# Q, K and V of two batches loaded two rows to a partition, in an attention and MLP kernel on one core

## The chip, the core and the metric

The kernel runs on one core of a Trainium2 chip. The core has TensorE (matrix products), VectorE, ScalarE, GpSimd and SyncE, which run side by side, each through its own list of instructions in order, and 16 DMA engines that serve the loads and stores which SyncE, ScalarE and GpSimd issue. Products are written to PSUM, eight banks here; all else lies in SBUF, with 128 partitions. The metric is the time on the device in microseconds (us), less is better.

## What is computed

First comes an attention with selected chunks: 4 batches, 8 heads, 768 positions, 64 values per head. K is cut into 24 chunks of 32 positions. An upper bound of a query's scores in a chunk is computed from the chunk's minimum and maximum of K, the six chunks with the highest bounds are kept (causally), and the softmax runs over these alone. The result goes through an MLP of 512 to 2048 to 512 with ELU.

```python
k_min = np.min(k_chunks, axis=3)
k_max = np.max(k_chunks, axis=3)
ub = np.sum(np.maximum(q[:, :, :, None, :] * k_min[:, :, None, :, :],
                       q[:, :, :, None, :] * k_max[:, :, None, :, :]), axis=-1)
ub = np.where(causal, ub, -1000000000.0)
top_chunks = np.argsort(ub, axis=-1)[..., -top_k:]
scores = scale * np.matmul(q, k.transpose(0, 1, 3, 2))
mask = sel & (pos[:, None] >= pos[None, :])
scores = np.where(mask, scores, -1000000000.0)
...
return np.matmul(attn, v).astype(np.float32)
...
h = x @ w_in
g = np.where(h > 0.0, h, alpha * (np.exp(np.minimum(h, 0.0)) - 1.0))
return (g @ w_out).astype(np.float32)
```

Inputs and output are float32; the kernel's products of scores, values and MLP are bf16.

## The kernel before

The work is cut into eight units of 384 rows. Units 0 and 1 hold the first halves of batches 0 and 1, in two steps of 192 positions: step p (`u == 0`) takes positions 0 to 191 of both batches, where no selection is needed because there are at most six chunks; step s (`u == 1`) takes positions 192 to 383. `prep_pair` (L379) loads and prepares them, `score_first` (L679) has the scores of step p, `attend_pair` (L708) the rest. Units 2 and 3 are the second halves of batches 0 and 1, units 4 to 7 the halves of batches 2 and 3; `prep` (L514) and `attend` (L770) do these. `mlp` (L868) then does one unit: 16 groups of four products with w_in (L875), for each group an exp on ScalarE (`e`, L882), a step on GpSimd or VectorE (`m`, L884) and one on VectorE (`g`, L888), and then three row tiles of 16 products with w_out (L899).

Every piece is an operation of a graph (`g.op`), with the engines that may run it. Which engine runs it, in which order on each engine, and in which buffer its result stands, is written out in two strings, `ORDER` (L39) and `PLACES` (L103): three characters for each operation (an engine and a number), one for each buffer. No scheduler decides on the chip: each engine does its list in order, and an instruction that waits holds back all behind it. There are 40 products with zeros (`fill`, L938) in the order that serve no result.

In batches 0 and 1 K and Q come in with positions on partitions, are transposed on TensorE into PSUM (L408 and L548; f32), and go on as follows. VectorE takes the minimum and maximum of each chunk from the bank into `kst` (`bounds`, L369, instructions at L372), and a subtraction follows (L375). K is copied as bf16 into `kt` (two heads, one above the other, on 128 partitions), and from there each head's 64 rows into `lhs` (`ka`). Step p uses `kt` and a copy of Q (`xt`) for its scores directly. In the other steps Q goes to `qt`, its positive part to `qr`, and each head's half to `rhs` (`qa`). `lhs` and `rhs` also hold, in rows 64 to 95, a pattern of chunks (`econst`) and the mask of the selection, so that one product of 96 rows gives a masked score. V is cast to bf16 into `vext` (`vcast`).

`select` (L590) multiplies `kst` with `qt` and `qr` (L603), turns the bounds on VectorE (L614), takes the eight largest of each row's visible chunks (L622), compares (L627), turns back (L631) and copies the result into `rhs` (`mk`).

Batches 2 and 3 do it in another way (`keys`, `bounds_batch`): K is cast into `kt` in another layout, transposed by a DMA into `lhs`, and its bounds come from a separate load `kc`.

The loads of K for step p are issued from ScalarE's queue and SyncE's, all other loads of Q, K and V from SyncE's, the weights from GpSimd's. In each, the last axis of the array in HBM, 64 float32 or 256 bytes, is one contiguous piece, as in these lines of `prep_pair`:

```python
src[b, h0:h1, t0 + T96 * x:t0 + T96 * (x + 1)].rearrange("h p d -> p h d")
```

V and Q of step p are put into the place of w_out (`stage`), which is loaded later.

Of the kernel before, what the change touches and what calls it, by code (L numbers as in the profile page):

```python
# [9 lines left out]
AOT = mybir.AluOpType  # L10
# [6 lines left out]
H = 8  # L17
S = 768
D = 64
# [20 lines left out]
D01A0sS0tS0xS0XS0wA0uS2hS0YA0VG0iD00S0ZS0yS2fS0+S0vD09G0jA0rD03G0eG04PjFA0WA02P1aS2kD1bS0BP11PjG  # L40
G0aG0cP18PjIS2iPjKS2gD0-S0zP0MP0DD19D15PjHG0bA05A0QP1tP0TD0ED17A1eD1cS2QP1uP1vD1dD0kD0FD10PjMP0K
P1kA1wPjOD0HD12P1oP1pG0dS2vA0UPjJD0OD0qD06A0LG0GA0SD0lG0nP1zP1qG0fD0mD13P2oG0RPjLA1xP1hD0pPjQD0N
A1rD0oP1SG0CP1jP1RP1lA1sA16P2BD2pA1iA1nG0AP1yD2qGmjP1AA2FPjNP1XD2DA1mP1OD1TGmkP1NA1CD2rD2CS3fP2w
S2RP2JA2sP1HPjPD1PP1EA1BG07GmlD2xP1DP1ID1JP20PjSD1UA2uPjRS2PD1QP29A2KP2aPjTS2OP1YG2HG0JD1FP33P1+
S2VPjVS2mD14S2ID1KD1GA1fA2yD1ZP3gD21P1VP25D2bG2EPjUD2LA2GP1LP26D22G0PD1-D1MP23D2cD27D24A1WD28A34
P3lPjWP2dD3nD3mA36PjXD3pPjZA2eD3oD3qD3rS2TPmuD2NAmvG2AD3hG37G3sDmwPmKPmGPmOP3JG3uPmCPj+PjYPmqD2S
AmLG0IAmHP2XAmPA2tGmmDmMDmNA35PmyG08AmrGmIGmnDmxS32P38DmJPk1Pk3G3tA2+Pj-DmQPk0G3vD2YPk5Pk2A2zPk7
A3KD2ZAmzP3HD39AmDPnmS4-DmRS4YDmEPniDmFA3cGmAPm-D3aG3dPmSA3IAm+AnnGmsDmBGn0DmtP3+Pk4GnoPn6AnjPna
GnkA3iG2-Dn1DnpD3kGmoP41An7Gn8G2lAnbDnlA31A40PnDPk6PmWAmTPk8GncDn9PnwA2MPn2G3bDndP3wA42AmXGmUDmV
A2nGmYPnePnxD1gDmZPk9P4lD3yP4FS50G30A3jS4+P4DAn3G43GmpG2WPnED3AA4mGn4D3xD3zD3BD2jP4jA4EP45PnqPnr  # L50
# [12 lines left out]
P7EA7nS7hP7DD7FA82D7GSnIPoQGc-D7XPkaD86D89D87S7HP8pP8BA8CPoRG8xPoSA8qG8nA8rPpsA8yA8dG8sSaxD7WD8k
D8jD8DSbADoTAptPpAA8ePpwPpoGaOG7YG8aPaPG8lG8oD88P8GD7ZApBGpCApxGpuPpcDpDSayPpgDpvGpyDpzPp0G8EApp
Pp8D8IG8bD8HAaQD8KPp4GpqDprA7-AaSApdAphGpiD8JDpjAp1PpkGpeDpfGp2G8gDp3AaTG8zD8LPpQAaRAp9SoVAp5PpI
GpaGp6ApRDpbDp7AplPpUGpSAb7A7+DpTSavPpEPpMPpYG8tPqcD8MApJSawApFSc+Pq0GpKSaCGpmDpLDpnApNGpGDpHAb9
G8NP93P8ZGcUG8OGbaSaUApZAb6ApVDp-P91Dp+PqdDpOP97DpWP96A94A92P8XG8fScLP8+DpPPq1A8-G95A8YDaWDbfA98
G99G8QP8TP8VG8PP9xP9wA90Pq2ScKP8RA8WA8UP9jP9rA9yDd0DpXP9bDaVDbhDboA8SA9kG9zP9fP9lA9sP9tP9aP9pA9m
P9hG8AA9uD9vP9nA9qDbvG8FSbBA9iDbDPq3P9RA9oP9HP9XP9WSaEGcTA9gD9cP9TP9FPqeSbbDq4D9dP9BA9YD9ZSf4A9I
DcXA9SA9GDaBP9ASazA9UP9ND9CP9PD9DP9JPahPadPa7PabSaXA9OG9VSb8A9QA9KPalP9LA9MGhxPakPqfDaZP9-DaYPaf  # L70
P9+AaePkcAbwPa3Da-Sq5ScRAa8Da+AacPkeAamDqgPq6Pa5Da0AagDa1Aa4S9EAaiSfgGb0Aa6DajGanPa9Pq7PaoAbgAaa
PapS9eSoUDbFDbdAbESa2DaqDarPb1GbGAb4Pq8Ab2PkdSasDfiAb5GbcAb3PbHDbIPq9PkfAbyDbJSbeGbiGcWDbKPkgSf5
DbLDbqDbMGcSSf9PqqPqSDbNPqmDbxAd1AqaAqrPqiAqTPquAbPGqsGbOPbYGqUAqnPbXPqCScPPreDqtDqVGqoGbRDqpPca
PbSDfhAqvDdcGqwPc9AqjAbQAbZGqkAqDGqEAbTDqlDqxPq-PqKArfDqFSf3Pr6ScNPcoPcnGrgPcCAq+AcbAr7GaDPcBDd8
PqyGr0AcpPcwSqhPr2AcDAqzPbUGr8SgbDrhDaFDr9Ar3PqWPcyDr1GcqAcxPciPqGDddGqAGr4AbVAczShkGb-Sf6Sf7PqO
Pc6ScYGcODr5AqHAqXGqIGd2AcjDqBProDd4DqJPckSgcDqYSg2Pc4ShlPraDcAAqLSfjGqMAc7ScVGbWGcEDqNPriPrjAcl
Ac5ArbDfRAd9PcFAqPAhwAd6DcmPc0GccPcrSf8PcsDc8PcGPb+Ad3DqZPceDrcPcdDd5DcHPrpGqQDqRPrqDcfDcgDrdPdg
PruPrrPrkPrlDc1GdfAfODctDc2SchGdbDcIGfPSc3DcuScvPrvScJPrIPs4PrUSqbDdiDflDdhPrASg1ArmDdkDdjSg9AfL
DdlPrwGdeSfQArsAs5DdmArVDdnPdJPdtSrnDfkSfxGrWGs6AhtPrQSfaDrXDdoPdIPrxGd7Pe6Pe7DfmArJAduGrKDs7PdF
ArBDrLAdKArRGrCGrSPrMDrDPdBDhCPdvPrESg4Ae8ArNDrOAdwArFGdqDrTDrPPsoGrGPdrPs0PsgAdCDdLPdDDryPdxAsp  # L80
AdGPdRShnAs1DrHGsqPrYSrzDsrAdsAshDe9DhuGsiPdzAdyShyDdaSgaAdEAdSPswPdVPs8ShvAdADdpDsjDdHArZGcQGs2
PdZPe1AsxPdNPdMSfXDs3GfJDr-PexAdWGsySfYDszPssDdOGfIAs9SfWPe3Ae2Dr+PdTAd-Pd+PeXDdPPeWDhEAdUPewAey
Ae0Ae4AeYPsAAstPdXPscPsBDsaPskSrtPefSfKDezAdYDfnGsuDsbDe5PeaAsdAslPeTPebGseSfeSg3PepDsfDecPelPsC
DedSfVAegPetPehDsvAemGsmGfoPfpPerAeUDsnDfsPenAeqShrPeHDfzSdQDfyDgdGfMDfZDg5AeuPsDPeJAesPeLAeoAei
GevPsMAeMAfqPejPeNPeBAeKAekPeFPeADfSPeRGg8AeOPsNAeSAeIPePDeCDeVGhAPsGGeZDeDDfbAeGPe-SeeAeQPe+PsH
PsIGfUAftDf0PsOPsJGg7Df1AgeSfuSeEDsEDfwSf2Pt2DfvPs-PtKDfrAsKGffDf-DfADfBDfCPfDPt6PsSAt3Dt4DfEAtL
As+SsLPsPGgfGtMDg6AfGAfFDf+Gt0Dt5DfHPghDt1PsWAsTGsUSfNDtNPtaPtiDsVShpAt7AsXDgiSfcPtqAtbDgjShmDgk
GhFGggDglDgmGt8GsYPtGPtOGtcAtjDsZPtmAsQDgnGfTGtkDt9AtrGgoPgxPgyAtHDtdGtsAgqPtyPgZDtlPgsPg-SsRDtt
PgWDhKAtnAgzDgAGgrGtoGgpGg0PteAtPDtpAgXPtCDtIAg+GtQPguPgUDtJAgtPgGAtfAgVDhGPtYDtgPtuAtzDtRAgvAtv
GtADh0SsFPtSAtDPgIDhzAgJDthPtZPtTDtwGgwPgMDtxAfdDtBAgHGgYPh8PgLPgBPhbDhHGhNAgNPh2PhcDgKPt-DtEPh6  # L90
PgCGgOAh9PgQPh1PgPDtFDhODgDAhdPu2Pu3Ah7GhaDgEPtUSgFDgRDh3DhLDgSDhePhfPhgGhJAhDAhPPhSPtVShBAhRAho
GhIDhhDhiPt+Pu4SgTShjGhMDh4Sh5DhTPu5PucGhsPuIPv4DhUDhVPukAtWAudAhqAuJDhWAu0DhXDhYStXDhZAv5PuwPi7
PugDu6GueGh-PibAulGuKAi8Su7AuxGumDuLPidPu8GuyDunPuoDufPiBAicAieAuhPi1Gv6PuADuzDv7Pi3GuiAu9AiCPuQ
GuaAupAuBPi5DujPixDubPusAi4Ai6DuqPuEPiDAi2GhQDurAuRPi9PiJDuSAiyAutPveGuCPiIAiEAuFPijDuDDuTDuGPii
AiaPivPifPuUAiwDuHPiFAigDuuPuYPuMDuvPvfAuVDihAikAuNDilPimPinGuWPizDuXAi0AiGPv0AiKPitDh+DuODuPAuZ
PjwAv1PirPvgAiuDioDipPi+Pj1Gu-Gv2AiAPjxGiLDiHPiTDu+PiRDv3Aj0Pj6PvhAisAj2PiNPiXPiMPj7Pj3AjyAiUAj4
DjzPv8PiVDviPjtAiSAj8DiOPiZSiqPv9DiPAiYPjfDj9Ai-PjrAiWGj5PjnPjbPjlPjaPjjAjuDjcAjgAjsPjhSiQAjoDjv
AjmDjdPvkPjpPvlSvjAjiAjqAjkPjBPjADjCSjeSu1PvaPvbPvmPvnAvoDjDSjEPvqAvcPvOPvyPvCPwaPvuAvzAvDGvAPv-
# [889 lines left out]
```

## Time and profile before

| | us |
|---|---|
| three runs | 289.12, 288.97, 287.55 |
| median | 288.97 |
| profiled execution | 288.57 |
| its span | 286.7 |
| mean granted clock of TensorE | 0.994 |

The page of the profile shows one execution. Its span runs from the first to the last instruction. A group of instructions is named by line, engine, operation and tile, with its count, its busy time, and the mean of one in ns; after the bar stands the idle time of the engine before it and what ended it. PEld is TensorE's loading of weights, beside its products. Products overlap on TensorE, so the mean duration of one is longer than the distance between two. A helper's line (L325, L327, L251, L309) stands for many operations; the tiles tell them apart. A row of the stretches gives the busy us of each engine with the count of its instructions, then TensorE's granted clock, the mean busy share of the 16 DMA engines (over 1 where packets overlap on one engine) and GB/s.

### The profile page before, as it was taken

To read this page: it belongs to the slowest core of one execution; us is meant where nothing else is said; L and a number is where in the kernel's file an instruction comes from. 1 tells how busy PE (TensorE), PEld (TensorE's weight loads), DVE (VectorE), ACT (ScalarE), POOL (GpSimd) and SP (SyncE) were. 2 spreads that over 40 slices of the span, in tenths; PEclk is the share of its full clock that TensorE was granted. 3 is DMA by queue.
4 is the path that set the end of the run, shared out by engine and by line. 5 is a ranking of instruction groups with operands and counts; after the bars stand their busy time and mean duration, and the time that the engine had idled before them with its cause. 6 is when DMAs were issued, how large, how long until landed. Compare 5 with 4: busy or idle time off the path is not lost.

```text
span 286.7 us, 6781 instructions
## 1 busy us (share of the span) xinstructions
PE 262.3 (91%) x2373; PEld 160.9 (56%) x2404; DVE 225.6 (79%) x608; ACT 195.9 (68%) x441; POOL 148.0 (52%) x285
## 2 busy tenths in 40 slices
PE   0669899999999999998899999998999989999995
PEld 0547565585556755565455455664465446665653
DVE  0397997769999999999989999698999867631850
ACT  2167587588999866898599278973488369892631
POOL 5065389743787568965379335335486442310520
PEclk9997999999999999999999999999999999999999
DMA  8999999969994679675789569973820430013003
GB/s 153 191 200 200 205 202 225 212 134 214 200 173 143 123 154 209 89 154 162 115 188 226 105 155 203 181 127 85 182 76 2 94 74 0 16 51 116 23 1 112
DMA packets 119714, 39.25 MB, mean 137 GB/s; under 512 B 111104, under 2 KB 115456, under 8 KB 119680
## 3 DMA queue, kind: packets, MB, share of 16 engines
q1 hardware_dynamic: 113072, 33.80, 59.7%
q0 software_dynamic: 3696, 4.19, 8.5%
q10 hardware_dynamic: 2912, 0.82, 1.5%
q8 instruction: 19, 0.31, 0.5%
q14 instruction: 15, 0.12, 0.1%
HBM read 30.41 MB, written 6.29 MB: 128 GB/s over the span
## 4 chain that ended last, share of the span: by engine, by line
PE 48%; DVE 28%; DMA 9%; ACT 5%; issue 5%; POOL 2%; SPq 2%; DVEq 0%; ACTq 0%
PE bank L875 15%; PE bank L899 13%; DVE km L491 6%; PE bank L785 5%; DVE gT L888 4%; DMA xt<-on 4%; PE bank L836 3%; DMA f<-in_k_dram 3%; ACT e L882 3%; PE bank L603 2%; DVE on L649 2%; DVE kst L372 2%; PE bank L408 2%; DVE thr L622 2%; PE bank L548 2%
## 5 line engine op out<-in xcount | busy, mean ns | idle before, releaser
L875 PE MATMUL bank<-xt,w_in_sb 128*128 128x384 bf16 x512 | 92.7, 326 | 3.9 <-DMA xt<-on 2.6
L884 POOL TENSOR_SCALAR m<-e 128x384 f32<-128x384 f32 x99 | 52.7, 541 | 73.4 <-ACT e L882 57.0
L899 PE MATMUL bank<-w_out_sb,gT 128*128 128x512 bf16 x338 | 86.4, 379 | 1.8 <-issue 0.2
L882 ACT ACTIVATE e<-bank 128x384 f32<-128x384 f32 x128 | 60.4, 497 | 27.0 <-PE bank L875 22.5
L888 DVE SCALAR_TENSOR_TENSOR gT<-bank,m 128x384 bf16<-128x384 f32 x128 | 66.5, 549 | 11.1 <-POOL m L884 9.4
L800 ACT ACTIVATE pt<-bank 128x384 bf16<-128x384 f32 (+1 forms) x144 | 68.6, 551 | 4.5 <-PE bank L785 2.2
L875 PEld LDWEIGHTS <-w_in_sb 128*128 128x128 bf16 x512 | 49.1, 98 | 38.5 <-issue 6.2
L899 PEld LDWEIGHTS <-gT 128*128 128x128 bf16 x368 | 34.5, 97 | 34.7 <-issue 1.6
L785 PE MATMUL bank<-rhs,lhs 96*128 96x384 bf16 (+2 forms) x240 | 45.1, 293 | 0.4
L491 DVE TENSOR_REDUCE km<-kc 96x64 f32<-96x1024 f32 x16 | 30.5, 1918 | 0.1
L785 PEld LDWEIGHTS <-lhs 96*128 96x128 bf16 x240 | 21.9, 97 | 15.2 <-issue 1.4
L817 POOL TENSOR_TENSOR pt<-pt,tri 128x256 bf16<-128x256 bf16 (+1 forms) x24 | 21.8, 915 | 12.9 <-ACT pt L800 12.1
L325 ACT ACTIVATE o<-bank 128x512 f32<-128x512 f32 (+2 forms) x16 | 8.5, 542 | 25.5 <-PE bank L899 21.2
L372 DVE TENSOR_REDUCE kst<-bank 128x12 f32<-128x384 f32 x32 | 16.3, 541 | 11.2 <-PE bank L408 9.4
L836 PEld LDWEIGHTS <-pt 128*128 128x128 bf16 x576 | 20.9, 97 | 5.7 <-DVE pt L817 1.3
L836 PE MATMUL bank<-vext,pt 128*128 128x65 bf16 x576 | 22.7, 193 | 1.5 <-DVE pt L817 0.7
L327 POOL CAST rhs<-qt 64x384 bf16<-64x384 f32 x32 | 16.5, 519 | 10.7 <-ACT qt L325 5.8
L884 DVE TENSOR_SCALAR m<-e 128x384 f32<-128x384 f32 x29 | 13.2, 457 | 10.4 <-ACT e L882 10.2
L649 DVE TENSOR_TENSOR on<-bank,rcp 128x384 bf16<-128x384 f32 (+1 forms) x40 | 19.4, 498 | 0.8
L804 ACT ACTIVATE pt<-bank 128x512 bf16<-128x512 f32 x24 | 14.6, 617 | 0.9 <-PE bank L785 0.4
L327 POOL COPY rhs<-selT 32x384 bf16<-32x384 bf16 (+1 forms) x18 | 11.7, 651 | 5.8 <-DVE selT L631 4.9
L647 DVE RECIPROCAL rcp<-bank 128x6 f32<-128x6 f32 (+1 forms) x40 | 6.7, 179 | 9.6 <-PE bank L836 6.8
(103 smaller groups left out, 308.4 us busy)
## 6 DMA issues: line engine op xcount, KB each, us to landing
out_dram<-o SPq DMA_DIRECT2D x21, 256.0 KB, 2.3
f<-in_v_dram SPq DMA_DIRECT2D x20, 256.0 KB, 4.4
f<-in_k_dram SPq DMA_DIRECT2D x18, 256.0 KB, 4.2
fx<-in_q_dram SPq DMA_DIRECT2D x32, 96.0 KB, 3.7
kc<-in_k_dram SPq DMA_DIRECT2D x8, 384.0 KB, 4.2
w_out_sb<-in_moe_w_out_dram POOLq DMA_DIRECT2D x4, 512.0 KB, 8.4
f<-in_q_dram SPq DMA_DIRECT2D x6, 256.0 KB, 6.6
w_in_sb<-in_moe_w_in_dram POOLq DMA_DIRECT2D x2, 512.0 KB, 9.8
```

The source lines that it names most:

```text
L327: eng[e].tensor_copy(out=dst, in_=src)
L372: g.op(("kmin", "kmax")[w] + tag, (DVE,), lambda e, w=w, op=op: nc.vector.tensor_reduce(out=cs(w), in_=src(), axis=AX.X, op=op), reads=[(b ...
L491: nc.vector.tensor_reduce(out=ap(km)[0:96, y, w], in_=ap(kc)[0:96].rearrange("p (w d) -> p d w", d=D), axis=AX.X, op=op), reads=[(kc, 0)], ...
L649: g.op("on" + tag, (DVE,), lambda e: nc.vector.tensor_tensor(out=ap(on)[:, 0:nt].rearrange("p q h d -> p h q d"), in0=view()[:, :, :, 0:D] ...
L785: nc.tensor.matmul(ap(banks[hd])[:, o + pc:o + pc + wd], lhsT=apl(ls, G)[0:96, pr, hd, P * kb:P * (kb + 1)], rhs=ap(rs)[0:96, hd, c0 - HS ...
L800: lambda e, hd=hd, pt=pt, banks=banks, wtot=wtot: nc.scalar.activation(out=ap(pt)[:, hd, PAD:PAD + wtot], in_=ap(banks[hd])[:, 0:wtot], fu ...
L836: nc.tensor.matmul(view()[:, hd, qi, :], lhsT=ap(pt)[:, hd, P * qi + off:P * qi + off + P], rhs=ap(vx[b])[:, kb, 2 * r + hd, :], start=(kb ...
L875: nc.tensor.matmul(ap(bank)[:, 0:HS], lhsT=w_in_sb[:, kk, P * fc:P * (fc + 1)], rhs=ap(xT[i, kk]), start=(kk == 0), stop=(kk == NKK - 1))
L882: g.op(f"e{i}.{fc}", (ACT,), lambda e, eb=eb, bank=bank: nc.scalar.activation(out=ap(eb), in_=ap(bank)[:, 0:HS], func=AF.Exp), reads=[(ban ...
L884: g.op(f"m{i}.{fc}", (POOL, DVE), lambda e, eb=eb, mb=mb: eng[e].tensor_scalar(out=ap(mb), in0=ap(eb), scalar1=-1.0, scalar2=1.0, op0=AOT. ...
L888: nc.vector.scalar_tensor_tensor(out=ap(gt), in0=ap(bank)[:, 0:HS], scalar=0.0, in1=ap(mb), op0=AOT.max, op1=AOT.min),
L899: nc.tensor.matmul(ap(bank), lhsT=ap(gts[fc])[:, P * tt:P * (tt + 1)], rhs=w_out_sb[:, fc, :], start=(fc == 0), stop=(fc == NFC - 1))
```

## The change

In batches 0 and 1 a partition takes two neighbouring positions of a head, 2p and 2p + 1, so that a piece in HBM is 128 float32 or 512 bytes. A transpose of 128 columns then gives, for one head, the even positions on partitions 0 to 63 and the odd ones on 64 to 127. From there on positions are kept in an order of their own, up to the rows of the output: within a group of 64 positions (units 0 and 1) or 128 (units 2 and 3) the even ones come first, then the odd.

- Loads: one per tensor, step and group of four heads (`[96, 4 x 128]`, 192 KB) in steps p and s; two per tensor and group of heads (128 and 64 partitions) in units 2 and 3. The four K loads of step p are on ScalarE's queue.
- K and Q: the two parities are copied from the bank straight into `lhs` (and in step p into `rhs`), each with gaps, as two copies; `kt` is no longer between. Step p's scores come from `lhs` and `rhs`. `kt` has two slots in place of four and serves batches 2 and 3 alone.
- Bounds: the minimum and maximum are taken over 16 positions of one parity, into a new tile `pk`; its halves are exchanged by two copies (`kx0`, `kx1`), and two operations (`km`, `kn`) join the parities into `kst`, once for each step or unit and batch (`both`), with one subtraction.
- V: each block of 32 or 64 partitions and parity goes into `vext` by a cast of its own (`values`), 72 casts of 4 x 64 elements in place of 14 of 8 x 64.
- Selection: for batches 0 and 1 the products run by head and parity at half the width; the turned bounds are written in two parts for each parity; a column of numbers (`early`) is added to three elements each, so that rows of an earlier chunk in the same block don't see the later one; the count of visible chunks follows the new order.
- Constants: the triangle masks are made in blocks of 32 or 64 rows for the new order (`triangle`: `trineg`, `trip`, `trih`), `econst` in two parts.
- Stores of units 0 to 3 write the rows of each group in two strided sets (`"(p j) n -> j p n"`).
- `ORDER` and `PLACES` are other strings throughout: engines, order and buffers of all operations are chosen anew.

```diff
+        kf, vf = Buf("f"), (stage[2 * b + G] if u == 0 else Buf("f"))
+        qf = stage[4 + 2 * b + G] if u == 0 else Buf("fx")
+        for n, buf, src in (("k", kf, k), ("q", qf, q), ("v", vf, v)):
+            dma(lambda buf=buf, src=src: (
+                    ap(buf)[0:T96, 0:512].rearrange("p (h x) -> p h x", h=4),
+                    src[b, hs, t0:t0 + QH].rearrange("h (p j) d -> p h (j d)", j=2)),
+                [(buf, 0)], [], f"ld{n}{tag}", (SP, ACT) if u == 0 and n == "k" else (SP,))
...
-        put("kt" + tag, lambda: rows2()[:, :, 0:QH], lambda: halves(bank), (ACT, DVE), [(bank, 0), (fixed, "kp")], [(kt, 0)])
-        for hd, half in enumerate((lo, hi)):
-            put(f"ka{hd}{tag}", lambda hd=hd: apl(lb, G)[lo, :, hd, t0:t0 + QH],
-                lambda half=half: rows2()[half, :, 0:QH],
-                (POOL, DVE, ACT), [(kt, 0)], [(lb, (0, u, hd, 2 * G + pr)) for pr in range(2)])
+        for jo, half in enumerate((lo, hi)):
+            put(f"ka{jo}{tag}",
+                lambda jo=jo: apl(lb, G)[lo, :, :, t0:t0 + QH].rearrange("d r h (g o w) -> d (r h) g o w", o=2, w=32)[:, :, :, jo],
+                lambda half=half: ap(bank)[half, 0:HS].rearrange("d (x g w) -> d x g w", x=4, w=32), (ACT, DVE), [(bank, 0)],
+                [(lb, (0, u, jo, 2 * G + pr)) for pr in range(2)] + [(lb, ("z", G))][:u])
...
+    def both(tag, b, pk, starts, n, c0, keys):
+        kst = ks[b]
+        part = [(pk, (s0, w)) for s0 in starts for w in range(2)]
+        for jo, (dst, src) in enumerate(((lo, hi), (hi, lo))):
+            put(f"kx{jo}{tag}", lambda dst=dst: ap(pk)[dst, 1, :, :, 0:n], lambda src=src: ap(pk)[src, 0, :, :, 0:n],
+                (DVE, POOL, ACT), part, [(pk, ("x", jo))])
+        for w, op in enumerate((AOT.min, AOT.max)):
+            g.op(("km", "kn")[w] + tag, (DVE,), lambda e, w=w, op=op: nc.vector.tensor_tensor(
+                out=ap(kst)[:, :, w, c0:c0 + n], in0=ap(pk)[:, 0, :, w, 0:n], in1=ap(pk)[:, 1, :, w, 0:n], op=op),
...
+    def values(tag, b, G, vf, rows, p0, pos):
+        for jo in range(2):
+            at = pos + rows * jo
+            kb, r0 = divmod(at, P)
+            vcast(f"v{tag}{jo}", lambda kb=kb, r0=r0: ap(vx[b])[r0:r0 + rows, kb, 4 * G:4 * G + 4, 0:D],
+                  lambda jo=jo: ap(vf)[p0:p0 + rows, 0:512].rearrange("p (h j d) -> p h j d", h=4, j=2)[:, :, jo],
+                  [(vf, 0)], [(vx[b], (kb, r0 >= 64, 2 * G + pr, jo)) for pr in range(2)])
...
+                    flat = ap(ubT)[:, y].rearrange("p b c -> p (b c)")
+                    for x in range(n):
+                        c0 = CHUNK * n * hd + (CHUNK + 2) * x + c_first + 1
+                        step = (CHUNK * 2 + 2) * n
+                        at = flat[:, c0:c0 + 2 * step + 1:step]
+                        nc.vector.tensor_scalar(out=at, in0=at, scalar1=early, scalar2=None, op0=AOT.add)
...
-BUFS = dict(f=8, fx=4, kc=1, km=1, kt=4, lhs=2, vext=2, rhs0=4, rhs1=5, kst=2, qt=5, qr=4, ubT=1, thr=2,
+BUFS = dict(f=8, fx=4, kc=1, km=1, kt=2, lhs=2, vext=2, rhs0=4, rhs1=5, kst=2, pk=1, qt=5, qr=4, ubT=1, thr=2,
...
+                def rows(row=row, n=c1 - c0):
+                    t = out[row:row + n, :]
+                    return t.rearrange("(p j) n -> j p n", j=2) if i < 4 else t
```

More of the change, by code (lines that the diff above doesn't have):

```diff
@@ L45 @@
[L45 to L50, printed above, removed]
@@ L276 @@
+    g.op("er", (POOL,), early_rows, writes=[(fixed, "er4")])
+    g.op("esum", (DVE,), lambda e: nc.vector.tensor_reduce(out=early, in_=early4, axis=AX.X, op=AOT.add),
+         reads=[(fixed, "er4")], writes=[(fixed, "er")])
     for half in range(2):
@@ L360, in open_batch @@
         lhs[b] = Buf("lhs")
+        if b < 2:
+            fill_const(f"lz{b}", (POOL, DVE), lambda: ap(lhs[b])[lo, :, :, QH:256], 0.0,
+                       [(lhs[b], ("z", G)) for G in range(NG)])
     def chunk_rows(b, G, half):
@@ L624, in select @@
+            need = [(ubT, ("t", x)) for x in range(2)] if b < 2 else [(ubT, ("t", hd))]
+            g.op(f"max{tag}{hd}", (DVE,), mx, reads=need, writes=[(ubT, hd), (thr, hd)])
         sb, sT = Buf("selb"), Buf("selT")
@@ L681, in score_first @@
         tag = f"{b}p{G}"
-        kt, qh = qq[b, G]
+        lb, rb = lhs[b], rhs[b, 0, G]
         pt = Buf("pt")
```

460 lines of the change are left out of this document (253 added, 207 removed).

## Prediction

> **What bounds the kernel now.** I read the page's first two parts, then the waits of the first 45 us, the chain in order of time at both ends, and last the busy times in seven stretches cut where the work changes.
>
> ```profile
> span 286.7 us, 6781 instructions
> PE 262.3 (91%) x2373; PEld 160.9 (56%) x2404; DVE 225.6 (79%) x608; ACT 195.9 (68%) x441; POOL 148.0 (52%) x285
> PE   0669899999999999998899999998999989999995
> ```
>
> TensorE is busy for 91% of the span, and the tenths show where it isn't: the first two or three slices.
>
> ```profile
> PE bank L408 <- DMA f<-in_k_dram: 8.7, 3, 6.3
> DVE kst L372 <- PE bank L408: 9.4, 1, 9.4
> ACT kt L325 <- PE bank L408: 7.9, 2, 7.6
> ```
>
> These are the longest waits of their engines (total us, times, longest): TensorE waits for the first K, and VectorE and ScalarE for TensorE.
>
> ```profile
> 0.82 2.96 DMA f<-in_k_dram
> 3.80 6.24 DMA f<-in_k_dram
> 10.08 1.38 PE bank L408 x7
> 31.35 0.85 PE L875 MATMUL bank<-xt,w_in_sb 128*128 128x384 bf16 x4
> 262.89 8.12 PE bank L875 x49
> 281.19 2.20 PE bank L855 x20
> ```
>
> In the chain a first 96 KB load of K takes 2.96 us; the fifth load on ScalarE's queue is issued only when the first has landed, and takes 6.24 us. So steady transposing begins at 10.08 and the first product of the MLP at 31.35. Near the end TensorE does MLP products back to back (8.12/49 = 166 ns each), and it finishes at 281.19 + 2.20 = 283.4.
>
> ```profile
> 0.00:13.40 13.40, 4.11 (x22) 3.52 (x23) 1.98 (x7) 1.67 (x3) 3.92 (x13) 1.00 1.08 172
> 13.40:31.40 18.00, 15.06 (x192) 10.96 (x193) 14.97 (x48) 11.88 (x26) 8.94 (x16) 0.91 1.27 199
> 31.40:51.50 20.10, 19.15 (x160) 11.89 (x161) 17.58 (x63) 14.84 (x33) 15.21 (x28) 1.00 1.23 216
> 51.50:81.50 30.00, 29.73 (x300) 19.43 (x301) 24.99 (x80) 23.93 (x54) 17.93 (x31) 1.00 1.00 186
> 81.50:156.80 75.30, 71.93 (x671) 43.84 (x678) 71.24 (x163) 63.02 (x149) 52.17 (x111) 1.00 0.76 156
> 220.00:286.70 66.70, 61.41 (x502) 36.00 (x509) 36.64 (x102) 38.33 (x86) 18.22 (x32) 1.00 0.20 52
> ```
>
> Columns: stretch, length, busy us of PE, PEld, DVE, ACT, POOL, granted clock, DMA share, GB/s. After 31.4 TensorE has work for 95 to 99% of the stretches up to 156.8, and VectorE for 95% of the longest. The DMA share is over 1 until 51.5. So the time is **the start of the MLP (31.35) plus some 252 us (to 283.4) in which TensorE, and VectorE close behind it, have no hole worth speaking of**. A change of the loads can gain only by starting the MLP earlier, or by having more done when it starts.
>
> **The loads.**
>
> ```profile
> DMA packets 119714, 39.25 MB, mean 137 GB/s; under 512 B 111104, under 2 KB 115456, under 8 KB 119680
> 20.00:30.00 10.00, 8.58 (x117) 6.72 (x118) 7.65 (x27) 6.84 (x15) 5.40 (x11) 0.83 1.22 200
> 210.00:220.00 10.00, 9.95 (x74) 6.03 (x74) 9.22 (x21) 8.77 (x19) 7.74 (x12) 1.00 0.15 54
> out_dram<-o SPq DMA_DIRECT2D x21, 256.0 KB, 2.3
> ```
>
> Q, K and V of batches 0 and 1 are 2 x 3 x 8 x 768 rows of 256 B: 36,864 of the 111,104 short packets. They become 18,432 packets of 512 B. No row shows such a packet. From 20 to 30 us, where rows of 256 B are loaded, a full share moves 200/1.22 = 164 GB/s, so a packet holds one of 16 engines 256 x 16/164 = 25 ns. From 210 to 220, mostly stores of 2 KB rows (256 KB over 128 partitions), it is 54/0.15 = 360 GB/s, 91 ns. On the line between them 512 B take 34 ns; the bounds are 25 (all cost per packet) and 50 (all per byte). With 34 the loads fall from 36,864 x 25/16 = 57.6 us of all engines to 39 (28.8 to 57.6). This lies beside other work, but for the first K. The Trainium skill speaks of this size: "DMA: Bandwidth & Descriptors", Specifications, gives 512 B as the least transfer for line rate, and says that below it the DMA reads, modifies and writes. An estimate from that page is that 512 B would cost no more than 256 B; the first K (next) would then land some 0.6 us sooner, and the sum below would be 286.3. The line through the two rows shows no step that large, but this trace holds no packet of 512 B that could settle it.
>
> **The start.** ScalarE's queue now issues four loads of 192 KB with no wait between them, and SP issues V and Q beside it. The first product needs one load of 192 KB where it needed two. It lands between 3.8 (the first row above, half as large) and 7.1 (0.82 + 6.24, 192 KB behind others); I take 5.0, nearer the first, since only one V load of 192 KB goes beside it. TensorE, VectorE and ScalarE thus begin 5.1 us earlier than 10.08. That isn't yet a gain: the 18 us up to the MLP had VectorE busy for 14.97 (83%), so engines, not loads, set their length.
>
> ```profile
> L703 ACT ACTIVATE pt<-bank 128x512 bf16<-128x512 f32 x8 | 4.4, 590 | 2.8 <-PE bank L695 2.8
> L325 ACT ACTIVATE kt<-bank 128x384 bf16<-128x384 f32 x4 | 1.8, 488 | 7.9 <-PE bank L408 7.9
> L325 ACT ACTIVATE vext<-f 128x512 bf16<-128x512 f32 x7 | 4.4, 626 | 0.0
> L325 ACT ACTIVATE kst<-bank 64x48 f32<-64x48 f32 x12 | 2.4, 202 | 1.8 <-PE bank L502 1.4 <-DVE kst L327 0.2
> L327 POOL COPY lhs<-kt 64x384 bf16<-64x384 bf16 x16 | 8.2, 516 | 1.7 <-ACT kt L325 1.1
> L338 POOL TENSOR_SCALAR vext<-f 128x512 bf16<-128x512 f32 x9 | 5.7, 630 | 0.0
> ```
>
> The casts of V are cut into blocks of 32 or 64 partitions: 72 of 256 elements in place of 14 of 512. On ScalarE such a cast costs between 202 ns (48 elements) and 626 (512); on the line between 48 and 384 elements, 380. Removed are the detour of K through kt (16 copies of some 490 ns, then 32 of mostly 516) and q's xt copies; K and Q of the first rows go from PSUM straight to lhs and rhs, two half-height copies of 384 elements for each.
>
> Ahead of the xt copy that releases the first MLP product, the new order has on ScalarE: 15 V casts (5.7), 11 lhs and 6 rhs copies from PSUM at 488 (8.3), 8 exps at 590 (4.7), and 9 others at about 490 or, for two of 96 elements, 240 (3.9). With one xt copy (0.5) that is **23.1 us, where ScalarE did 11.88** from 13.4 to 31.4. Its in-order queue starts with a V cast at 5.0. Fully packed, the MLP starts at 28.1; at VectorE's 83%, at 32.8. ScalarE is now the fullest engine, so I take 92%: 5.0 + 23.1/0.92 = 30.1. That is **-1.2 us** (-3.2 to +1.5).
>
> ```profile
> L272 POOL TENSOR_SCALAR_AFFINE_SELECT trineg<-trineg 128x384 bf16<-128x384 bf16 x1 | 0.5, 512 | 0.1
> L272 POOL TENSOR_SCALAR_AFFINE_SELECT trineg<-trineg 128x128 bf16<-128x128 bf16 x1 | 0.3, 303 | 0.0
> w_in_sb<-in_moe_w_in_dram POOLq DMA_DIRECT2D x2, 512.0 KB, 9.8
> ```
>
> GpSimd has some 30 instructions ahead of its first load of w_in, at 0.3 to 0.63 us: masks in 32-row blocks, fills, and six V casts, four of which wait for their loads. Behind them stands w_in. 30 at 0.4 are 12 us from 0.8 on; with some waiting it leaves near 16 and lands near 26, with 4 us to spare. If the V loads came 5 us later, it would be the next thing late.
>
> **More done at that point.** The new order puts all 16 min/max reductions of the first rows ahead of the MLP.
>
> ```profile
> L372 DVE TENSOR_REDUCE kst<-bank 128x12 f32<-128x384 f32 x12 | 6.3, 535 | 11.2 <-PE bank L408 9.4 <-ACT kt L325 1.6
> L614 DVE STREAM_TRANSPOSE ubT<-bank 128x192 f32<-128x192 f32 x8 | 2.7, 361 | 0.1
> L614 DVE STREAM_TRANSPOSE ubT<-bank 128x384 f32<-128x384 f32 x8 | 4.3, 565 | 0.4 <-PE bank L603 0.3
> L620 DVE MEMSET ubT<- 128x1 f32 x8 | 0.5, 59 | 0.1
> L375 DVE TENSOR_TENSOR kst<-kst 128x12 f32<-128x12 f32 x5 | 0.8, 160 | 0.1
> ```
>
> Before, 12 stood there: four at 535 ns, 2.1 us of VectorE that later stretches don't have. TensorE, not VectorE, is the fuller engine after 31.4 outside the long stretch, so I count **-0.9** (-2.1 to 0).
>
> **The selection gets longer.** For (0, 1) and (1, 1) each, two transposes of 565 ns become four of 361 or so, and eight additions of three elements appear, between 59 and 160 ns, say 110: 0.3 + 0.9 = 1.2 us in a chain from scores to mask, 2.4 for both. MLP products cover it while VectorE has room (24.99 of 30 us); with that cover gone it is all paid. I take **+0.4** (0 to +2.4). Selections (0, 0) and (1, 0) get half the additions, inside the start's bounds.
>
> **The rest.**
>
> ```profile
> lhs<-kt SPq DMA_TRANSPOSE x12, 3.4
> ```
>
> MLP and score products are as many as before, and so are the 40 fillers; the stores keep rows of 2 KB. For batches 2 and 3 kt has two slots in place of four, so every third cast of K waits until a transposing load (3.4 us) has read the first, and the copies behind it on its engine wait too: nothing while MLP products cover it, up to 3.4 us at each of four groups if they don't, of which I count none. After the start ScalarE has some 5 us more (72 casts against 14, less the copies), GpSimd about 7. From 51.5 to 156.8 ScalarE idles 18 us and GpSimd 35: nothing, +3 if the cover fails where VectorE is at 95%.
>
> The profiled execution took 288.57: its span of 286.7 and 1.9 around it. 288.57 - 1.2 - 0.9 + 0.4 = **286.9 us**. Against the median of 288.97 that is -0.7%.
>
> **Rivals.** *The whole lead comes through.* The engines pack fully and nothing later gives it back: -3.2 for the start, -2.1 for the reductions: 283.3. For it: the lead at the first product is 5.1 us. Against: ScalarE's 23.1 us.
>
> *ScalarE becomes the late one.* It takes every V cast in order, each waiting for its load, while the exps stand behind them. It filled 66% (11.88 of 18) before, VectorE 83%. Under 23.1/26.35 = 88% the MLP starts later than 31.35. At 83% that is +1.5, and with the selection uncovered +2.4 the time is 292.5; the reductions' -0.9 makes it 291.6.
>
> *It doesn't matter.* Half the packets, but the loads were hidden from 13.4 on, and the earlier start is used up by the casts to the tenth: 31.35 again, 288.6.
>
> **How the numbers follow.** 0.5% (1.4 us) is about what a measurement of this kernel can tell from no change: 287.5 to 290.4. My forecast gets 0.36 (0.24 faster, 0.10 same, 0.02 slower), the whole lead 0.18 (all faster), no effect 0.16 (0.04, 0.06, 0.06), ScalarE late 0.30 (0.01, 0.02, 0.27). Together faster 0.47, same 0.18, slower 0.35. The forecast's own range is 284.5 to 289. To hold 8 in 10 it must reach into both sides: 282.0, a little under the whole lead (the K landing at 3.8), to 293.0, over the late ScalarE (the +3 partly paid).
>
> **What would show it.** Right: first transposing near 5, the first MLP product near 30, ScalarE over 85% busy between, and TensorE without new holes after it; the mean DMA share of the first 50 us lower. Wrong: the MLP's start after 31.4; a wait of TensorE on an xt copy or on w_in longer than 1 us; VectorE waiting on ScalarE's lhs or rhs copies; or an unchanged start with TensorE's holes after 150 us grown, which would put the cause in the new order and not in the loads.

## The result, and the profile after

The changed kernel takes 328.04 us (median of four runs, 325.34 to 329.76), the kernel before beside it 288.76 (287.55 to 289.12): a ratio of 1.136, 95% interval 1.127 to 1.145. That is far above the forecast of 286.9, and outside its range of 282.0 to 293.0. The profiled execution took 327.07, of which 325.4 are its span. One run of those that follow (309.65 us, with the outermost dimension 4) lies 1.7% above the fastest of its kernel and is left out of that kernel's median and ratio.

Its page, the same rows as shown of before, with the DMA row and the chain's shares besides:

```profile
span 325.4 us, 7222 instructions
...
PE 283.8 (87%) x2519; PEld 168.8 (52%) x2548; DVE 228.9 (70%) x634; ACT 212.0 (65%) x481; POOL 163.8 (50%) x332
...
PE   4887999998879899995859976997959899999995
...
PEclk9999999999999999998968999799987999999999
DMA  8979995574445999657897763974553342011202
...
PE 42%; DMA 20%; DVE 15%; ACT 7%; POOL 7%; issue 5%; SPq 3%; POOLq 0%; DVEq 0%; ACTq 0%
```

And the rows of before that were not needed until now:

```profile
PEclk9997999999999999999999999999999999999999
DMA  8999999969994679675789569973820430013003
...
PE 48%; DVE 28%; DMA 9%; ACT 5%; issue 5%; POOL 2%; SPq 2%; DVEq 0%; ACTq 0%
...
kc<-in_k_dram SPq DMA_DIRECT2D x8, 384.0 KB, 4.2
...
xt<-on SPq DMA_TRANSPOSE x24, 2.6
```

TensorE now has holes in the middle (slices of 5 to 8 tenths), the granted clock falls there, and the share of DMA in the chain has doubled, while the DMA engines' mean share is lower than before, not higher. So transfers are late although the 16 engines together have room. The stretches, cut at the same times as in the prediction (one more, 156.8 to 220, is added), show where:

```profile
0.00:13.40 13.40, 8.43 (x44) 6.11 (x45) 8.27 (x26) 6.39 (x14) 9.42 (x30) 1.00 0.99 226
13.40:31.40 18.00, 14.65 (x226) 10.89 (x224) 14.79 (x59) 17.41 (x39) 15.15 (x36) 1.00 0.93 167
31.40:51.50 20.10, 18.63 (x207) 12.07 (x208) 18.05 (x58) 16.64 (x37) 15.04 (x31) 1.00 1.17 217
51.50:81.50 30.00, 28.78 (x278) 17.43 (x280) 19.37 (x76) 18.49 (x43) 12.55 (x44) 1.00 0.51 118
81.50:156.80 75.30, 66.58 (x601) 38.53 (x607) 56.79 (x125) 59.72 (x140) 46.15 (x82) 0.98 0.77 133
156.80:220.00 63.20, 52.72 (x418) 29.74 (x421) 44.73 (x119) 37.51 (x84) 30.93 (x52) 0.92 0.80 130
```

Up to 51.5 nothing is lost: the start is as before. From 81.5 to 156.8 VectorE is busy for 56.79 us where before had 71.24, ScalarE for 59.72 where it had 63.02, TensorE for 66.58 (71.93): all engines wait. The chain of waits has these pieces of over 4 us between 80 and 230 (start, length, what):

```profile
85.35 7.27 DMA f<-in_k_dram
103.57 8.29 DMA f<-in_q_dram
139.89 7.20 DMA kc<-in_k_dram
156.37 8.37 DMA out_dram<-o
200.54 4.94 DMA f<-in_v_dram
212.28 8.48 DMA fx<-in_q_dram
229.42 8.51 DMA kc<-in_k_dram
```

A store took 2.3 us in the kernel before; here one takes 8.37, and loads of K and Q, which don't touch the output, take as long. The first such piece starts at 85.35, 21 us after the first store is issued (64.2). The waits say the same from the other end (total us, times, longest): ScalarE waits for a buffer `o` that a store still reads, VectorE for `kc`.

```profile
ACT o L355 <- DMA out_dram<-o: 9.9, 3, 5.7
DVE km L531 <- DMA kc<-in_k_dram: 9.8, 3, 5.1
```

Before, the first of these was shorter, and VectorE's idle time ahead of the reductions of `kc`, the last number of its row, was 0.1:

```profile
ACT o L325 <- DMA out_dram<-o: 3.5, 2, 2.6
...
L491 DVE TENSOR_REDUCE km<-kc 96x64 f32<-96x1024 f32 x16 | 30.5, 1918 | 0.1
```

**Reading.** The stores of units 0 to 3 changed their shape: `"(p j) n -> j p n"` makes the destination `[2, rows/2, 512]`, with an outermost dimension of 2. In rows of 2 KB nothing changed, and the prediction goes by these alone. Theory A was that such a store is served by only two of the 16 DMA engines, and that all else which these two carry, a part of every load, waits behind it. The rivals were the new order, ScalarE, and the jumps between the rows in HBM.

### The profile page after: what moved, and what is told of

It is laid out like the page before. It is cut to its first block, busy times and chain, and to the rows that moved or that the text cites. A ratio compares the mean times of both kernels' runs of the same rounds, so it can differ in the third digit from the quotient of the medians.

```text
span 325.4 us, 7222 instructions
## 1 busy us (share of the span) xinstructions
PE 283.8 (87%) x2519; PEld 168.8 (52%) x2548; DVE 228.9 (70%) x634; ACT 212.0 (65%) x481; POOL 163.8 (50%) x332
## 2 busy tenths in 40 slices
DMA packets 101129, 39.28 MB, mean 121 GB/s; under 512 B 74084, under 2 KB 96868, under 8 KB 101092
## 4 chain that ended last, share of the span: by engine, by line
PE 42%; DMA 20%; DVE 15%; ACT 7%; POOL 7%; issue 5%; SPq 3%; POOLq 0%; DVEq 0%; ACTq 0%
PE bank L957 14%; PE bank L981 12%; DMA kc<-in_k_dram 5%; DVE km L531 3%; PE bank L867 3%; DVE gT L970 3%; ACT e L964 3%; DMA fx<-in_q_dram 3%; DMA out_dram<-o 3%; DMA f<-in_q_dram 3%; PE bank L918 2%; SPq L343 2%; DMA f<-in_k_dram 2%; DMA lhs<-econst 2%; POOL m L966 2%
## 5 line engine op out<-in xcount | busy, mean ns | idle before, releaser
L957 PE MATMUL bank<-xt,w_in_sb 128*128 128x384 bf16 x512 | 98.3, 338 | 7.7 <-ACT o L355 4.7
L981 PE MATMUL bank<-w_out_sb,gT 128*128 128x512 bf16 x339 | 88.1, 383 | 2.5 <-DVE gT L970 0.8
L957 PEld LDWEIGHTS <-w_in_sb 128*128 128x128 bf16 x512 | 50.7, 101 | 44.3 <-issue 14.8
L867 PE MATMUL bank<-rhs,lhs 96*128 96x384 bf16 (+2 forms) x240 | 47.3, 301 | 8.5 <-ACT o L355 2.9
L867 PEld LDWEIGHTS <-lhs 96*128 96x128 bf16 x240 | 22.5, 100 | 25.1 <-issue 12.5
L355 ACT ACTIVATE o<-bank 128x512 f32<-128x512 f32 (+1 forms) x15 | 8.5, 579 | 35.7 <-PE bank L981 11.3
L918 PE MATMUL bank<-vext,pt 128*128 128x65 bf16 x576 | 23.1, 195 | 1.6 <-DVE pt L899 0.9
L357 POOL CAST rhs<-qt 64x384 bf16<-64x384 f32 x38 | 18.9, 500 | 1.4
L899 POOL TENSOR_TENSOR pt<-pt,tri 128x256 bf16<-128x256 bf16 (+1 forms) x17 | 15.1, 897 | 8.2 <-ACT pt L882 6.5
L365 POOL TENSOR_SCALAR vext<-f 64x256 bf16<-64x256 f32 (+2 forms) x30 | 14.1, 471 | 8.6 <-DMA f<-in_v_dram 7.0
L355 ACT ACTIVATE lhs<-bank 64x384 bf16<-64x384 f32 x29 | 13.8, 481 | 6.3 <-PE bank L444 3.9
L402 DVE TENSOR_REDUCE pk<-bank 128x24 f32<-128x384 f32 x32 | 16.3, 545 | 1.9 <-PE bank L596 1.3
```

Source lines behind the costliest of these rows:

```text
L355: nc.scalar.activation(out=dst, in_=src, func=AF.Copy)
L357: eng[e].tensor_copy(out=dst, in_=src)
L867: nc.tensor.matmul(ap(banks[hd])[:, o + pc:o + pc + wd], lhsT=apl(ls, G)[0:96, pr, hd, P * kb:P * (kb + 1)], rhs=ap(rs)[0:96, hd, c0 - HS ...
L918: nc.tensor.matmul(view()[:, hd, qi, :], lhsT=ap(pt)[:, hd, P * qi + off:P * qi + off + P], rhs=ap(vx[b])[:, kb, 2 * r + hd, :], start=(kb ...
L957: nc.tensor.matmul(ap(bank)[:, 0:HS], lhsT=w_in_sb[:, kk, P * fc:P * (fc + 1)], rhs=ap(xT[i, kk]), start=(kk == 0), stop=(kk == NKK - 1))
L981: nc.tensor.matmul(ap(bank), lhsT=ap(gts[fc])[:, P * tt:P * (tt + 1)], rhs=w_out_sb[:, fc, :], start=(fc == 0), stop=(fc == NFC - 1))
```

## The experiments

**Each store cut in two (e1).** The changed kernel, with the even and the odd rows of each store of units 0 to 3 as a store of its own, so that the outermost dimension is 32 or 64:

```diff
...
-                    return t.rearrange("(p j) n -> j p n", j=2) if i < 4 else t
...
+                    t = out[row:row + n, :].rearrange("(p j) n -> p j n", j=2)
+                    for y in range(2):
+                        eng[e].dma_start(out=t[:, y], in_=ap(ob)[c0 + n // 2 * y:c0 + n // 2 * (y + 1)])
```

> The changed kernel; each store of units 0 to 3 is cut into two, one for the even and one for the odd output rows, so that 32 or 64 rows are its outermost dimension in place of 2. Order, buffers, rows written and all else stay; SyncE issues 18 more stores. Theory A (a store whose outermost dimension is 2 runs on two of the 16 DMA engines, takes 8 us in place of 2.3, and holds up the loads behind it on these two): 282 to 290 us, stores land in 2 to 3 us again, and the 256 B loads of 100 to 170 us take some 4 us in place of up to 8. Theory B (the new order makes SyncE's queue wait: 29.0 us on VectorE for xt, 27.9 on GpSimd for lhs, 13 for econst): 318 to 330, with the same waits. Theory C (16 us more of ScalarE, 16 of GpSimd): 315 to 328, ScalarE over 90% in the stretches where TensorE has holes.

Measured: 296.5 us (296.3 to 297.5, four runs), ratio 1.028 (1.024 to 1.032). Of the loss of 39 us, 31.5 are gone with this edit alone. In its list of DMA issues (count, KB, median us to landing) the stores are short again:

```profile
out_dram<-o SPq DMA_DIRECT2D x24, 64.0 KB, 2.4
```

But 8 us were left, more than the expectation allowed.

**The other way round (e2).** The kernel before, with nothing but the shape of these stores changed:

```diff
-                dma(lambda ob=ob, c0=c0, c1=c1, row=row: (out[row:row + c1 - c0, :], ap(ob)[c0:c1]),
+                def rows(row=row, n=c1 - c0):
+                    t = out[row:row + n, :]
+                    return t.rearrange("(p j) n -> j p n", j=2) if i < 4 else t
+                dma(lambda ob=ob, c0=c0, c1=c1, rows=rows: (rows(), ap(ob)[c0:c1]),
```

> The kernel before, with only the stores' destination of units 0 to 3 written as in the change, [2, 32 or 64, 512]; the rows of its output are therefore permuted. Theory A: the loss shows without the rest of the change, 310 to 330 us. Theories B and C: no loss, 287 to 291.

Measured: 324.32 us (322.34 to 324.83, five runs), ratio 1.125 (1.120 to 1.129): the one line costs 36 us in a kernel that has none of the rest of the change. Pieces of its chain:

```profile
92.50 8.64 DMA out_dram<-o
111.19 8.61 DMA xt<-on
145.27 8.09 DMA out_dram<-o
```

The stores take 8 us, and a transposing load of `xt` between them, 2.6 us in the list of before, takes 8.61.

**How many engines (e8, e9).** It could still be the distance between rows, 4 KB in place of 2, and not the number of engines. The same edit of the kernel before, with 4 and 16 for the 2 in `j=2`, sets the two apart: the distance grows with the number, and so do the engines.

> The kernel before, its stores of units 0 to 3 written with an outermost dimension of 4 instead of 2 (each destination [4, rows/4, 512], the output's rows permuted within a store). Theory A, the outermost dimension of an access sets how many of the 16 DMA engines a store runs on: four engines take half as long as two, and most of the 36 us of the version with two (324.3) are gone: 290 to 305, stores in the list of DMA issues at 3 to 5 us. Rival, it is the jumps between rows in DRAM (here 8 KB from one row to the next, with two 4 KB) and not the number of engines: as slow as with two or slower, 320 to 335.

> The same with an outermost dimension of 16 (rows of a store 32 KB apart from one to the next). Theory A: all 16 engines, no loss: 288 to 291. Rival, the jumps between rows: 320 to 340.

| outermost dimension | median us | ratio (95% interval) |
|---|---|---|
| 2 | 324.32 | 1.125 (1.120 to 1.129) |
| 4 | 305.84 | 1.061 (1.055 to 1.067) |
| 16 | 288.51 | 0.999 (0.998 to 1.001) |

With 16 the rows of a store are 32 KB apart and nothing is lost; with 4, half of what 2 costs is lost (6.1% against 12.5%; the expectation's upper end was 305). Theory A holds, and the jumps fall.

The traces also count the engines. A transfer reports its landing to a semaphore in steps, and a trace has the time of each step. Before, every transfer has 16: 3,008 steps for 188 transfers. In the kernels with split stores and with 16 in place of 2 it is 16 each as well. The changed kernel has 2,870 steps for 194 transfers, which is 16 for each but the 18 stores of units 0 to 3, and 3 for each of these; with 2 in the kernel before (14 such stores) it is 3 again, with 4 it is 5. One step of the 3 or 5 comes mostly about 1 us after the issue, long before the rest; the 2 or 4 that are left are read here as one for each engine. The steps also show who waits. In the changed kernel 31 of the 176 other transfers have 14 steps together and the last two over 1 us later; the load of Q issued at 103.57 has 14 steps within 2.99 us and the last two after 8.27 and 8.29. The kernel before has 2 such transfers of 188 and the one with split stores 1 of 212, all before 41 us; the kernel before with its stores changed to 2 has 19 of 174. So two engines of the 16 are late, and the others are not. One part of the expectation for 4 missed: it put these stores at 3 to 5 us, and by their last step they took 6.7 (median; 8.1 with 2, 3.4 with 16).

This is also what the Trainium skill states: "DMA: Bandwidth & Descriptors", section "Why a DMA increments its semaphore by 16 and not by 1", says that a DMA runs on the largest number of engines, 16 at most, that divides the slowest dimension of both its accesses. The three times agree with it, and so do the numbers of steps. The prediction draws on that page for the price of 512 B and not on this section. It says too that, for DMAs issued by SyncE or ScalarE, these are the lowest-numbered engines, so that all such stores would share the same two; no run here shows which they were.

**Transposes of two sizes (e3, e4).** For the 8 us that were left I compared TensorE's groups. Before, the transposes of K and Q for units 2 and 3 are one group; in the kernel with split stores they are two, of 128 and of 64 partitions in turn:

```profile
L548 PE MATMUL bank<-ident_f,f 128*128 128x128 f32 x48 | 7.3, 278 | 0.6 <-DVE on L649 0.6
```

```profile
L595 PE MATMUL bank<-ident_f,f 128*128 128x128 f32 x32 | 10.0, 312 | 0.0
L596 PE MATMUL bank<-ident_f,f 64*128 64x64 f32 x32 | 8.7, 272 | 0.0
```

48 in 7.3 us became 64 in 18.7, on an engine that has work for nearly all of the time. The timeline (start, us, engine, line) shows that they no longer overlap. Three of before, and the product that comes next:

```profile
60.26 0.49 PE L548 MATMUL bank<-ident_f,f 128*128 128x128 f32 x3
60.58 0.53 PE L757 MATMUL bank<-vext,pt 128*128 128x65 bf16 x12
```

The kernel with split stores:

```profile
53.23 0.27 PE L595 MATMUL bank<-ident_f,f 128*128 128x128 f32 x1
53.44 0.27 PE L596 MATMUL bank<-ident_f,f 64*128 64x64 f32 x1
53.64 0.33 PE L595 MATMUL bank<-ident_f,f 128*128 128x128 f32 x1
...
55.02 1.90 PE L981 MATMUL bank<-w_out_sb,gT 128*128 128x512 bf16 x8
```

Three start within 0.32 us there, 107 ns apart; here eight need 1.79 us, 224 ns each, the start of one hardly before the end of the one ahead. That was theory B, against theory C, that the rest was the new order's. Two edits of the kernel with split stores: the two large ones first and then the two small, or all four large, the second reading the whole tile of which the upper 64 rows serve nothing, its superfluous columns being written over by the next. (e4 keeps the loop over `hd` and the line of `c0`, which the cut below takes out for e3 alone.)

```diff
-                for hd in range(2):
-                    c0 = P * (2 * pr + hd)
-                    nc.tensor.transpose(ap(bk)[:, QH * hd:QH * hd + P], ap(src[0])[:, c0:c0 + P], ident_f)
-                    nc.tensor.transpose(ap(bk)[:, QH * hd + P:QH * (hd + 1)], ap(src[1])[0:64, c0:c0 + P],
-                                        ident_f[0:64, 0:64])
+                for x, p1 in enumerate((P, 64)):                                        # e3
+                    for hd in range(2):
+                        c0 = P * (2 * pr + hd)
+                        nc.tensor.transpose(ap(bk)[:, QH * hd + P * x:QH * hd + P * x + p1],
+                                            ap(src[x])[0:p1, c0:c0 + P], ident_f[0:p1, 0:p1])
...
+                    for x in range(2):                                                  # e4
+                        nc.tensor.transpose(ap(bk)[:, QH * hd + P * x:QH * hd + P * x + P],
+                                            ap(src[x])[:, c0:c0 + P], ident_f)
```

> The changed kernel with the split stores (296.5), and in each transposing of K or Q of rows of 512 B behind the start the two of 128 partitions first, then the two of 64 (before: 128, 64, 128, 64). Theory B, what is left over is TensorE's: alternating tiles of 128 and 64 partitions start 224 ns apart (8 in 1.79 us from 53.23 to 55.02), where before's transposes, all of 128, start about 107 ns apart (3 in 0.32 us at 60.26). With half the alternations gone 32 of the 64 start 107 ns behind the one ahead: 3.7 us less, 292.8 (291 to 295). If a tile of 64 partitions is slow by itself: no gain, 296 to 297. Theory C, the rest comes from the new order and from SP's queue, which stands still from 14.8 to 27.8: no gain, 295.5 to 297.5.

> As the one with grouped transposes, but all four are of 128 partitions: the second reads the whole tile, whose upper 64 rows belong to nothing, and the columns that they give are written over by the next or never read. Theory B: 64 starts at 107 instead of 224 ns, 7.5 us less of TensorE, which is full: 289 (287.5 to 291), TensorE's busy time near 267 instead of 274.5. A tile of 64 slow by itself: the same 289. Theory C: no gain, 295.5 to 297.5.

Measured: 292.84 us for the grouped ones (292.27 to 293.26, four runs), ratio 1.014 (1.011 to 1.018); 290.49 for the full ones (289.65 to 293.05, ten runs), ratio 1.007 (1.004 to 1.009). Eight of them in the middle, grouped, with the product that comes next:

```profile
60.73 1.28 PE L596 MATMUL bank<-ident_f,f 128*128 128x128 f32 x8
61.94 1.04 PE L981 MATMUL bank<-w_out_sb,gT 128*128 128x512 bf16 x4
```

and all full:

```profile
59.57 1.04 PE L596 MATMUL bank<-ident_f,f 128*128 128x128 f32 x8
60.45 1.03 PE L981 MATMUL bank<-w_out_sb,gT 128*128 128x512 bf16 x4
```

Eight now take 1.21 and 0.88 us up to the next product in place of 1.79 (the first eight of these two kernels are slower, 1.35 and 1.20). Added up over all 64, from each start to the next on TensorE, it is 14.3 us with split stores, 9.8 grouped and 7.4 full: 4.5 and 6.8 less, where the kernel gained 3.7 and 6.0. Theory B holds, for the full ones at the size put for it: 107 ns were expected, and their median distance is 109, as before the change. The distances also rule out that a tile of 64 is slow by itself: in e3, 64 behind 64 starts after 113 ns (median), 64 behind 128 after 203.

**ScalarE at the start (e5), fewer transposes (e6), both (e7).** The first product of the MLP that waits for `xt` comes at 31.56, though the first transpose comes at 4.7 instead of 10.08. ScalarE's timeline in the changed kernel says why:

```profile
4.42 0.42 ACT L355 ACTIVATE vext<-w_out_sb 32x256 bf16<-32x256 f32 x1
8.72 0.49 ACT L355 ACTIVATE lhs<-bank 64x384 bf16<-64x384 f32 x1 [3.88 <-PE bank L444]
...
31.03 0.48 ACT L355 ACTIVATE xt<-bank 128x384 bf16<-128x384 bf16 x1
```

It waits 3.88 us for a transposed bank, and behind the waiting copy stand casts of V whose loads have landed before its wait ends. After it there is no hole: 17.41 of 18 us in the second stretch. The fifth experiment takes four of these casts (1.7 us) ahead of the copy, in the kernel of e4; the sixth loads the second part of K and of Q with the odd heads in the upper 64 partitions, so that one transpose serves two heads (48 in place of 64, for 8 more issues on SyncE); the seventh does both.

```diff
+MOVES = [('v0p010', 'ka10p0'),
+         ('v0p011', 'ka10p0'),
+         ('v1p000', 'ka10p0'),
+         ('v1p001', 'ka10p0')]
```

```diff
+                nc.tensor.transpose(ap(bk)[:, 0:HS].rearrange("q (h w) -> q h w", h=2)[:, :, P:QH],
+                                    ap(src[1])[:, P * pr:P * (pr + 1)], ident_f)
```

> The kernel with split stores and transposes of 128 partitions (290.49), with four of ScalarE's casts of V (1.7 us), whose loads have landed by then, moved ahead of its first copy of K from PSUM, into the 3.9 us (4.84 to 8.76) in which it waits for TensorE. Theory D, ScalarE sets the start of the MLP: its work was 22.7 us as predicted, but it can only begin at 8.76 instead of 5.0 and has no hole from there to the xt copy at 31.03. Then xt and the MLP come 1.3 to 1.7 us earlier (first product on the whole xt near 30.1 instead of 31.6), the time is 289.0 (288.5 to 289.8). Rival, VectorE (88% busy from 10 to 20) or the chain of scores and exps sets it: the MLP's start moves under 0.5 us, 290.0 to 290.8.

> The kernel with split stores and transposes of 128 partitions (290.49); the second load of K and of Q puts the odd heads into the upper 64 partitions, so that three transposes do for four (48 instead of 64, as many as before the change) for 8 more issues on SP. Theory B, TensorE is full from 31 us on: 16 starts at 107 ns less, 1.7 us, 288.8 (288.2 to 289.8). If the waits for VectorE and GpSimd set the time now: 290 to 291.

> Both of these edits. If theories B and D hold and add up: 287.3 (286.5 to 288.5), 0.5% under the kernel before. If one of the gains is given back at a later wait: 288.5 to 290.

| kernel | median us | ratio (95% interval) |
|---|---|---|
| e4, from which they start | 290.49 | 1.0066 (1.0038 to 1.0094) |
| e5, casts ahead | 289.81 | 1.0024 (0.9999 to 1.0048) |
| e6, three transposes | 291.15 | 1.0074 (1.0050 to 1.0098) |
| e7, both | 290.02 | 1.0040 (1.0017 to 1.0062) |

The last three ran on one chip, e4 on another, so e4 stands beside them by its ratio. From e6 to e7 the casts gain 1.1 us (the difference of the means is 1.0, with a 95% interval of 0.4 to 1.6), from e4 to e5 0.4% of ratio, 1.2 us, though those two intervals overlap: a little less than the 1.3 to 1.7 that theory D asked for, and more than its rival allowed. All three medians lie at or just above the upper ends of what was expected for them. The first stall is mostly gone and the start moves. From e7, ScalarE's timeline:

```profile
4.40 1.27 ACT L360 ACTIVATE vext<-w_out_sb 32x256 bf16<-32x256 f32 x3
6.84 0.85 ACT L360 ACTIVATE vext<-w_out_sb 32x256 bf16<-32x256 f32 x2 [1.17 <-DMA w_out_sb<-in_v_dram]
8.65 0.49 ACT L360 ACTIVATE lhs<-bank 64x384 bf16<-64x384 f32 x1 [0.96 <-PE bank L449]
...
29.80 0.48 ACT L360 ACTIVATE xt<-bank 128x384 bf16<-128x384 bf16 x1
```

`xt` is copied at 29.80 instead of 31.03, 1.2 us for 1.7 moved; in e6, which has the other edit alone, the copy stands at 31.16. (In the profile of e5 itself the granted clock was 0.81 to 0.88 from 10 to 31 us, and the copy stood at 31.14; its start can't be read there.)

The three transposes gained nothing (e5 to e7: 0.2 us more), although they take 6.4 us of TensorE from start to start in place of 7.4. Theory B's reason, that TensorE is full, no longer held for the whole of e4. Its chain of waits from 124 to 136 us, in part:

```profile
124.62 1.15 POOL pt L899
125.83 0.84 POOL rhs L357
...
133.31 1.16 POOL pt L899
134.47 0.59 POOL vext L365
135.07 0.63 POOL pt L899
```

GpSimd sets the pace there (masks on `pt`, copies to `rhs`, a cast of V), and a lead of TensorE that comes before it is waited away. No version tried is faster than the kernel before; the nearest, e5, can't be told from it.

## Why the prediction was wrong

**The step that failed** is the half sentence "the stores keep rows of 2 KB", with which they were costed at nothing. The rows did stay; the outermost dimension became 2. That is 31.5 us in the changed kernel (e1) and 36 in the kernel before (e2). Its size could have been estimated from rows that stood there, given the number of engines, which no row of before tells: a row of 2 KB took an engine 91 ns, and units 0 to 3 store 4 x 384 = 1,536 of them. On 16 engines that is 96 rows or 8.7 us each, on two engines 768 rows or 70 us each. These two also carry their sixteenth of all else, and its share was 0.83 of the time between 51 and 157 us (mean of the rows quoted in the prediction: 1.00 for 30 us and 0.76 for 75). Some 70 us more, between 64 and 230, hardly fit beside it. This is an estimate; that two engines were late is seen in the steps, and which two is not. What the reader should keep is that no mean shows it: the DMA row averages over 16 engines, and here it fell.

**A second step** was left out: "MLP and score products are as many as before, and so are the 40 fillers" counts every product but the transposes. 48 became 64, half of them of another height, and a TensorE that was said to be full from 31 us on must pay for each. 64 x 224 - 48 x 107 ns is 9.2 us; taking part of it away returned 6.0 (e4). With this term alone the sum would have been 286.9 + 9.2 = 296.1, slower than before. That e1 took 296.5 is nearer to it than the sum deserves, by luck: the 1.2 us that it counts for the start did not come.

**The start.** That transposing begins near 5 was right (4.73 in the changed kernel's chain), and so was ScalarE's work: 23.1 us forecast up to the end of the `xt` copy; measured are 0.42 from 4.42 on and, with hardly a hole, 8.72 to 31.51, 23.2 in all. But "its in-order queue starts with a V cast at 5.0" overlooked the second instruction: a copy that waits for TensorE until 8.72. So 5.0 + 23.1/0.92 should have been 8.7 + 22.8 = 31.5, and the gain of 1.2 us was none. e7 supports it: with the hole partly filled the copy starts at 29.8. On the start the rival "It doesn't matter" was right (31.35 forecast, 31.56 measured), though for the reason that I had given to the late ScalarE.

**The loads** came out near the forecast: the packets fell from 119,714 to 101,129, and SyncE's queue, 59.7% of 286.7 us before, holds 52.9% of 294.7 with split stores: 171 us of all engines against 156, 15 less where 18.6 were forecast. With split stores a packet of 512 B took 34.2 ns on average and one of 256 B 21.8 (22.8 before), where the prediction had 34 and 25; its other estimate, that 512 B cost no more than 256 B, did not come out. The saving brought nothing, since no wait for these loads stands in the chain of the kernel with split stores after the start. That the DMA share of the first 50 us would be lower held too. The first load of w_in was issued at 15.2, near the forecast of 16, and landed 6.3 us later, at 21.6 instead of 26; it was not in the way.

**The rivals** had the right side, slower, at 0.35, but none had the mechanism; the range's upper end was made of ScalarE's and the selection's prices. Among the signs that would prove it wrong the prediction names "an unchanged start with TensorE's holes after 150 us grown, which would put the cause in the new order": the start was unchanged and the holes grew, from 80 us on, and yet the cause was an access pattern and not the order, as e2 shows, which has the old order.

**Open.** The longer selection, the earlier reductions and the two slots of `kt` were not tried by themselves. Between e5 and the kernel before, 0.2% with an interval that holds zero, nothing is shown that is left to explain; what GpSimd's and ScalarE's extra casts cost in the middle was read from the chain of e4 and not shown by an edit.

## What to carry to other kernels

When a rearrangement touches a DMA, read both access patterns dimension by dimension, outermost first, and not only the length of a row: 2 or 4 in the outermost place cost the engines that it left out here, and not the stores alone paid but transfers behind them. Count the transposes as you count the products, by the distance between their starts, and keep neighbours on TensorE of one height. And where an in-order engine starts early, look at its second instruction too.

## What the runs showed of the hardware

- A store of 2 KB rows whose destination has an outermost dimension of 2, 4 or 16 made the whole kernel 12.5%, 6.1% and 0% slower; its landing was reported in 3, 5 and 16 steps. With 2, other transfers had 14 of their 16 steps on time and two up to 5.3 us later. A distance of 32 KB from row to row cost nothing.
- f32 transposes start 109 ns apart (median) where all have 128 partitions, before the change and in e4; where 128 and 64 alternate, the one of 64 starts after 259 ns and the next of 128 after 202, 224 ns on average over eight. In e3 64 behind 64 starts after 113 ns. I had not expected that a change of height from one tile to the next sets the price.
- With the holes came a lower clock; that they caused it was not tested. The granted clock of TensorE was 0.92 from 156.8 to 220 us, where it idled for 10 of 63 us (before, with hardly a hole after the start, it was 0.994 over the whole), and the 512 products of L957 took 338 ns on average instead of 326, 5.6 us in all (98.3 against 92.7):

```profile
L957 PE MATMUL bank<-xt,w_in_sb 128*128 128x384 bf16 x512 | 98.3, 338 | 7.7 <-ACT o L355 4.7
```

```profile
L957 PE MATMUL bank<-xt,w_in_sb 128*128 128x384 bf16 x512 | 92.7, 326 | 1.7 <-DMA xt<-on 1.1
```

The first is of the changed kernel, the second of the one with split stores.
